# Decode attention with a gated MLP on one core: passing the opening barrier from a block late in the program

## The chip, the cores and the metric

One core of a Trainium2 chip. The metric is the device time of one execution in microseconds (us). A profiled execution also has a span, counted from the first recorded instruction; over 55 executions the time is 2.0 us above the span. In this document "last wo data" is the end of the last packet of the last weight load in the trace's packet records, and "first data" the start of the first packet of the first K load.

The engines, as the profile of before shows them: PE runs the matmuls (4482), DVE and ACT work on vectors (311 and 184 instructions), POOL fills constants (20), SP issues the loads. Each has a program of its own in the kernel; they meet at an opening barrier and then by semaphores. The packet records, sampled every microsecond from 5 to 1260 us, have exactly 16 packets under way at once, the fetches of code (queues 8 and 14) among them: one for each of 16 DMA engines.

## The reference, cut to what matters

```python
def reference(A_x, A_k_cache, A_v_cache, A_wq, A_wo, B_x, B_w1, B_b1, B_w2, B_b2, gate_w):
    ...
    x = A_x
    g = _sigmoid((x * gate_w).sum(-1, keepdims=True))
    a = _A_ref(x, A_k_cache, A_v_cache, A_wq, A_wo)   # 2 batches, 16 query heads on 8 KV heads, 32768 keys of 256
    b = _B_ref(x, B_w1, B_b1, B_w2, B_b2)             # 448 -> 1792 -> 448, gelu
    return g * a + (1 - g) * b
```

One new token per batch. The caches are 2 x 8 x 32768 x 256 bf16 values each, 537 MB together; the rest is small.

## The kernel before: the parts that matter

K and V tiles of 8.4 MB pass through a ring of three slots. SP's first K load is put into the entry block, ahead of the barrier; the five programs follow in blocks of their own.

```python
        entry = nc.main_func.blocks[-1]
        n0 = len(entry.instructions)
        engs["sp"].eng = nc.sync
        first_load(engs["sp"])
        ins = entry.instructions
        at = next(i for i, x in enumerate(ins) if x.engine == mybir.EngineType.SP and type(x).__name__ == "InstDrain")
        entry.instructions = ins[:at] + ins[n0:] + ins[at:n0]
        with nc.Block("main") as block:
            ...
            block.tensor(lambda eng: run("pe", eng))
```

PE's program is short in code: the 32 tiles are one loop, whose pass has a K half (scores) and a V half (weighted sum), each under a condition. Behind the loop come the last V tile in three pieces and the tail: 28 small matmuls for w2 (line L603) and 64 for wo (L781), which wait for wo's five pieces.

```python
            def tile(i):
                def k():
                    S(i)
                    next_slot()

                def v():
                    PV(i - LAG)
                    next_slot()

                E.iff(i < NTILES, lambda e: e.If_lt(R["i"], NTILES), k)
                E.iff(i >= LAG, lambda e: e.If_lt(R["n"], NTILES - 1), v)
                ...
            E.rep(NTILES + LAG - 1, tile)
            ...
            PV_pieces()
            ...
            TT()
            do_FB()
            E.wait("dve", "at")
            for i in range(len(WOP) - 1):
                FIN(i)
```

## Time and profile before

| | before |
|---|---|
| time, median of the first 3 executions | 1271.87 us (1271.77, 1271.87, 1272.60) |
| span of the profiled one | 1269.6 us |
| HBM read | 547.43 MB, 431 GB/s over the span |
| code fetches in the run | 16 KB at 52.9 us (q8), 8 KB at 140.3, 1226.1 and 1240.6 us (q14), 16 KB at 1265.8 us (q8) |
| last wo data | 1266.79 us |

How to read it: the DMA share was 1.00 from 50 to 1220 us, at 434 GB/s, and 0.98 from 1260 to 1265 us, and the last wo data ended 2.8 us before the end of the span. So look for what delays the DMA engines, or for what follows the last landing. The lines are shown in the prediction.

### The profile page before, as it was taken

How to read it: one execution, taken by the hardware profiler on the slowest of the kernel's cores; microseconds unless marked ns; L12 is line 12 of the kernel's file. 1: busy time of each engine (PE TensorE's matmuls, PEld its weight loads, DVE VectorE, ACT ScalarE, POOL GpSimd, SP SyncE). 2: the span in 40 equal slices, each digit the busy share in tenths (PEclk: the TensorE clock that was granted, in tenths of full speed). 3: DMA queues.
4: the chain of work that ended last, by engine and by line, in shares of the span. 5: the costliest groups of instructions: out<-in, count | busy, mean ns of one | idle time of the engine just before them, and what ended most of it. 6: DMA issues, size and time to landing. Idle time of an engine off the chain costs nothing.

```text
span 1269.6 us, 12680 instructions
## 1 busy us (share of the span) xinstructions
PE 870.9 (69%) x4482; PEld 179.4 (14%) x1938; DVE 688.8 (54%) x311; ACT 44.7 (4%) x184; POOL 4.6 (0%) x20
## 2 busy tenths in 40 slices
PE   0978677766688565785766877666876657857678
PEld 0211111111111111111111111111111111111113
DVE  4676536755356563556735467453575635656351
ACT  0100000000000000000000000000000000000000
POOL 1000000000000000000000000000000000000000
PEclk9889888877988788888778878888877789877789
DMA  9999999999999999999999999999999999999998
GB/s 407 451 429 429 432 429 438 438 440 432 429 432 432 429 434 440 436 438 429 432 432 429 432 440 438 436 432 429 434 429 429 440 438 438 432 429 432 432 428 367
DMA packets 11110, 547.50 MB, mean 431 GB/s; under 512 B 1369, under 2 KB 1633, under 8 KB 2145
## 3 DMA queue, kind: packets, MB, share of 16 engines
q1 hardware_dynamic: 10948, 547.43, 99.8%
q8 instruction: 2, 0.03, 0.0%
q10 hardware_dynamic: 156, 0.01, 0.0%
q14 instruction: 4, 0.02, 0.0%
HBM read 547.43 MB, written 0.00 MB: 431 GB/s over the span
## 4 chain that ended last, share of the span: by engine, by line
DMA 55%; PE 24%; DVE 14%; issue 6%; SPq 0%; ACT 0%; ACTq 0%
DMA ring<-in_A_k_cache_dram 51%; DVE ring L958 12%; PE ps_s L666 12%; PE ps_o L666 11%; DMA ring<-in_A_wo_dram 3%; DVE mx L962 1%; DMA PT<-in_gate_w_dram 1%; PE ps_m L721 0%; PE ps_m L716 0%; DVE gmax L964 0%; PE ps_o L577 0%; PE ps_o L445 0%; DVE gmx L968 0%; PE ps_o L548 0%; PE ps_o L582 0%
## 5 line engine op out<-in xcount | busy, mean ns | idle before, releaser
L958 DVE STREAM_TRANSPOSE ring<-ring 128x4096 uint32<-128x4096 uint32 x128 | 557.4, 4412 | 305.2 <-DMA ring<-in_A_k_cache_dram 304.9
L666 PE MATMUL ps_s<-ring,Abd 128*128 x2048 | 519.7, 416 | 221.1 <-DVE ring L958 220.9
L666 PE MATMUL ps_o<-ring,PT 128*24 x2048 | 271.5, 421 | 10.1 <-issue 9.9
L666 PEld LDWEIGHTS ps_s<-ring,Abd 128*128 x1024 | 106.2, 104 | 640.7 <-issue 637.7
L975 DVE STREAM_TRANSPOSE PT<-pexp 128x1024 bf16<-128x1024 bf16 x16 | 19.9, 1245 | 117.5 <-PE ps_o L666 117.5
L726 PE MATMUL ps_f<-o_sb,selg 128*32 128x257 f32 x30 | 15.5, 621 | 91.0 <-DVE o_sb L991 91.0
L666 PEld LDWEIGHTS ps_o<-ring,PT 128*24 x544 | 46.5, 90 | 214.9 <-issue 213.1
L962 DVE TENSOR_REDUCE mx<-ps_s 128x1 f32<-128x1024 f32 x16 | 19.6, 1225 | 63.5 <-PE ps_s L666 63.5
L874 ACT ACTIVATE negm<-ps_m 128x1 f32<-128x1 f32 x16 | 2.7, 171 | 1132.9 <-PE ps_m L721 1132.9
L991 DVE TENSOR_REDUCE o_sb<-ps_o 128x256 f32<-128x2048 f32 x15 | 34.4, 2291 | 0.5
L989 DVE TENSOR_TENSOR ps_o<-ps_o,mask 128x2048 f32<-128x2048 f32 x15 | 34.3, 2290 | 0.0
L716 PE MATMUL ps_m<-ident_f,mx 128*1 128x128 f32 x32 | 6.1, 270 | 22.3 <-DVE mx L962 22.3
L972 DVE COPY ls<-lsum 128x1 f32<-128x1 f32 x16 | 2.5, 154 | 33.4 <-ACT pexp L878 33.4
L548 PE MATMUL ps_o<-ring,xT 128*32 128x512 bf16 x16 | 5.6, 567 | 20.4 <-issue 20.4
L868 ACT COPY Abd<-qrep 32x16 bf16 (+1 forms) x128 | 19.5, 199 | 0.6
L619 PE MATMUL ps_s<-zeros 1*128 1x512 bf16 x32 | 15.7, 590 | 5.2 <-ACT Abd L868 2.7
L878 ACT ACTIVATE pexp<-ps_s,negm 128x1024 bf16<-128x1024 f32 x16 | 17.8, 1114 | 1.7
L619 PE MATMUL ps_o<-zeros 1*128 1x512 bf16 x64 | 17.3, 392 | 0.5 <-DVE o_sb L984 0.5
L726 PEld LDWEIGHTS ps_f<-o_sb,selg 128*32 128x32 f32 x30 | 2.7, 138 | 104.8 <-issue 104.8
L721 PE MATMUL ps_m<-ones_f,gmx 1*128 1x1 f32 x32 | 6.5, 270 | 11.1 <-DVE gmx L968 11.1
L964 DVE TENSOR_REDUCE gmax<-ps_m 1x2 f32<-1x128 f32 x16 | 4.5, 278 | 8.8 <-PE ps_m L716 8.8
L1005 DVE TENSOR_SCALAR o_sb<-ps_o,mask 128x256 f32<-128x256 f32 x1 | 0.5, 483 | 15.7 <-PE ps_o L666 15.7
(92 smaller groups left out, 81.4 us busy)
## 6 DMA issues: line engine op xcount, KB each, us to landing
ring<-in_A_v_cache_dram SPq DMA_DIRECT2D x1, 4096.0 KB, 27.2
ring<-in_A_v_cache_dram SPq DMA_DIRECT2D x2, 2048.0 KB, 33.9
ring<-in_A_wq_dram SPq DMA_DIRECT2D x1, 3072.0 KB, 28.8
ring<-in_B_w_dram SPq DMA_DIRECT2D x1, 1568.0 KB, 28.3
ring<-in_A_wo_dram SPq DMA_DIRECT2D x1, 1568.0 KB, 31.7
ring<-in_B_w_dram SPq DMA_DIRECT2D x1, 1344.0 KB, 32.3
ring<-in_A_wo_dram SPq DMA_DIRECT2D x1, 1008.0 KB, 33.7
ring<-in_A_wo_dram SPq DMA_DIRECT2D x1, 560.0 KB, 34.5
```

The costliest lines, as they stand in the source:

```text
L619: E.ins(lambda e: e.matmul(o, zeros[0:1, :], zero_x, start=True, stop=False, skip_group_check=True))
L666: return e.add_instruction(mybir.InstMatmult(name=f"I-{nc.next_id()}", engine=mybir.EngineType.PE, ldweights=None if load else False, ins= ...
L716: E.ins(lambda e: e.matmul(ps_m[0:1, C_MXT:C_MXT + P], mx[:, :], ident_f[:, :], start=True, stop=True), key=("M1", g))
L721: E.ins(lambda e: e.matmul(ps_m[:, C_BC:C_BC + 1], gmx[:, :], ones_f[0:1, 0:1], start=True, stop=True), key=("M2", g))
L726: E.ins(lambda e: e.matmul(ps_oa, selg[:, :], o_sb[:, :], start=False, stop=False, skip_group_check=True), key=("OT", g))
L868: E.ins(lambda e, o=o, Q=Q, c=c: e.copy(o[:, :, c:c + 2], qrep[32 * Q:32 * Q + 32, :, bass.ds(E.dyn(2 * g, 2), 2)]), key=(("A", g) if (Q = ...
L878: E.ins(lambda e: e.activation(pexp[:, :].rearrange("p (r i a) -> p i r a", r=CR, i=2), ps_s[:, :].rearrange("p (i r a) -> p i r a", i=2, ...
L958: E.ins(lambda e: e.transpose(k_words(idx, blk), k_words(idx, blk)), key=("T", idx, blk))
L962: E.ins(lambda e: e.tensor_reduce(mx[:, :], ps_s[:, :], AX.X, ALU.max), key=("MX", g))
L975: E.ins(lambda e: e.transpose(PT[:, :], pexp[:, :]), key=("PT", g))
L989: E.ins(lambda e: e.tensor_tensor(p, p, mb, ALU.mult), key=("OM", g))
L991: E.ins(lambda e: e.tensor_reduce(o_sb[:, 0:Dh], ps_o[:, :].rearrange("p (n d) -> p d n", d=Dh), AX.X, ALU.add), key=("OS", g))
```

## The change

The intent: four engines jump at once to a block that stands late in their program, pass the opening barrier there and jump back, so that late code is fetched at the start and not in the middle of the run or at its end.

```diff
+        def gate(eng, before):
+            ...
+            mine = [x for x in entry.instructions if of(x)]      # the engine's Drain, EventSemaphore, UnconditionalBranch
+            assert len(mine) == 3
+            name = f"gate_{eng.name}"
+            rest = [x for x in entry.instructions if not of(x)]
+            entry.instructions = rest + [mybir.InstUnconditionalBranch(
+                name=f"I-{nc.next_id()}", engine=eng, ins=[], outs=[], target=name)]
+            blocks = list(f.blocks)
+            at = next(i for i, b in enumerate(blocks) if b.name == before)
+            bb = mybir.BasicBlock(name=name, instructions=mine)
+            f.blocks = blocks[:at] + [bb] + blocks[at:]
+            ...
+        spots = [(ET.SP, names[-1]), (ET.Activation, names[last(ET.Activation)]), (ET.DVE, names[last(ET.DVE)]),
+                 (ET.PE, names[last(ET.PE) - 8])]
+        for eng, before in spots:
+            gate(eng, before)
```

SP, ACT and DVE get the block at their ends. PE gets it eight blocks before its end.

More of the change, by code (lines that the diff above doesn't have):

```diff
@@ L1073, in bass_gated_mix__gqa_block_cached__dense_activation_gelu__decode_kernel @@
             block.vector(lambda eng: run("dve", eng))
+        def gate(eng, before):
+            f = nc.main_func
+            of = lambda x: x.engine == eng and type(x).__name__ in ("InstDrain", "InstEventSemaphore", "InstUnconditionalBranch")
+            mine = [x for x in entry.instructions if of(x)]
[8 more added lines that the diff above has]
+            f.blocks = blocks[:at] + [bb] + blocks[at:]
+            nc.bb_map[name] = bass.BassBasicBlock(nc, bb, [eng], parent=nc.bb_map[entry.name])
+        blocks = list(nc.main_func.blocks)
+        names = [b.name for b in blocks]
+        ET = mybir.EngineType
+        last = lambda eng: max(i for i, b in enumerate(blocks[:-1]) if b.instructions[-1].engine == eng) + 1
+        spots = [(ET.SP, names[-1]), (ET.Activation, names[last(ET.Activation)]), (ET.DVE, names[last(ET.DVE)]),
+                 (ET.PE, names[last(ET.PE) - 8])]
+        for eng, before in spots:
+            gate(eng, before)
 _INS = ['A_x', 'A_k_cache', 'A_v_cache', 'A_wq', 'A_wo', 'B_x', 'B_w1', 'B_b1', 'B_w2', 'B_b2', 'gate_w']
```

## The prediction

> **What bounds the kernel now.** I read the page from the top down: first the DMA and GB/s rows of the 40 slices, then the queues, then the chain that ended last.
>
> ```profile
> DMA  9999999999999999999999999999999999999998
> GB/s 407 451 429 429 432 429 438 438 440 432 429 432 432 429 434 440 436 438 429 432 432 429 432 440 438 436 432 429 434 429 429 440 438 438 432 429 432 432 428 367
> ...
> q1 hardware_dynamic: 10948, 547.43, 99.8%
> q8 instruction: 2, 0.03, 0.0%
> ...
> q14 instruction: 4, 0.02, 0.0%
> HBM read 547.43 MB, written 0.00 MB: 431 GB/s over the span
> ...
> DMA 55%; PE 24%; DVE 14%; issue 6%; SPq 0%; ACT 0%; ACTq 0%
> ```
>
> The DMA row never falls below nine tenths until the last slice: the kernel streams the two caches once, and the stream is the bound. The two "instruction" rows are what this change is about: fetches of code during the run, on queues 8 and 14, next to the data of queue 1. They are 0.05 MB, so by bytes they are nothing.
>
> The table of busy time by stretch and the chain of waits show the same for the end:
>
> ```profile
> 50.00:1220.00 1170.00, 817.64 (x4081) 161.26 (x1665) 651.70 (x258) 37.38 (x165) 0.00 (x0) 0.83 1.00 434
> ...
> 1265.00:1266.00 1.00, 1.00 (x22) 0.71 (x16) 0.00 (x0) 0.00 (x0) 0.00 (x0) 1.00 0.69 249
> 1266.00:1267.00 1.00, 0.68 (x13) 0.36 (x11) 0.00 (x0) 0.00 (x0) 0.00 (x0) 1.00 0.09 33
> ...
> 1232.03 34.92 DMA ring<-in_A_wo_dram
> 1266.95 0.04 issue
> 1267.00 0.57 PE ps_f L781 x8
> 1267.57 0.02 issue
> 1267.59 0.38 DVE pexp L1044
> ```
>
> In a row of the first kind the last two numbers are DMA share and GB/s. The share is 1.00 for 1170 us and then falls to 0.69 and 0.09 in the last two microseconds: most of the 16 DMA engines are done and one or two are late. The last piece of wo waits for these, then come eight matmuls, a copy and the output. So the end is **the slowest DMA engine plus 2.8 us** (1266.8 to the span's 1269.6).
>
> To see which engine is late and why, I went to the packet records of the trace (start, duration, queue, size). They carry no engine number, but an engine's next packet starts 3 ns before the end of its previous one is noted, so the records sort into 16 chains. Result: from the first packets (1.04 to 1.87 us, one per engine) to 1265 us no chain has a hole over 60 ns, except at four instruction fetches:
>
> ```
> fetch starts us  took us  bytes  queue   what its engine's chain lost
>   52.89          1.06     16384  q8      1.55 us (hole 1.05, next 64 KB packet 2.92 instead of 2.42)
>  140.34          0.33      8192  q14     0.97 us (hole 0.31, next packet 3.08)
> 1226.06          0.31      8192  q14     0.69 us (hole 0.31, next packet 2.80)
> 1240.56          0.31      8192  q14     0.31 us
> 1265.79          1.09     16384  q8      on an engine that had finished its data, it seems
> ```
>
> As each engine always has backlog (K tiles land 43.8 us after their issue, though one needs 19.4 us), what a chain loses is never caught up. At the end the two chains that lost 1.55 and 0.97 us are the last: 1266.79 and 1266.66, the others 1265.1 to 1266.02. The weight of a fetch is therefore not its bytes over 431 GB/s but the full delay of one engine out of 16, for which all wait.
>
> [...]
>
> **The change part by part.**
> (1) It moves no data, no arithmetic and no wait. The order of instructions differs by one branch each on PE, DVE, ACT and SP: their three opening barrier instructions now stand late in their programs, so an engine jumps there, passes the barrier, and jumps back. The first K load stays in the entry block, ahead of SP's jump, at 0.00.
> (2) Cost at the start: four branches (a DVE or PE branch took 0.05 to 0.21 us) and the wait for up to four fetches under the first K load, an estimate of 2 to 5 us for the barrier, because a queued packet of 64 KB takes 2.42 us (3.0 to 3.5 the first time). What hangs on the barrier:
>
> ```profile
> 0.00 0.41 SPq L481 DMA_DIRECT2D ring<-in_A_k_cache_dram  x1
> ...
> 0.82 0.80 SPq L495 DMA_DIRECT2D ring<-in_A_wq_dram  x2
> ...
> 2.74 42.97 SPq L517 DMA_DIRECT2D ring<-in_A_k_cache_dram  x2
> ...
> 19.50 0.61 DVE L918 TENSOR_TENSOR gp_sb<-pexp,PT 2x448 f32<-2x448 bf16 x1 [9.38 <-DMA PT<-in_gate_w_dram]
> ...
> 22.30 17.42 DVE L958 STREAM_TRANSPOSE ring<-ring 128x4096 uint32<-128x4096 uint32 x4 [0.52 <-DMA ring<-in_A_k_cache_dram]
> ```
>
> wq is issued at 0.82 but its first packets run at 21.1, after the first K tile: 20 us of slack. The third K tile is issued at 45.7 and first needed at 52.9, and what releases its slot follows wq's landing, not the barrier. gate_w would land later by the barrier's delay, moving the first transposes from 22.3; they end at 39.7, and DVE's next thing on the path is the h copy at 45.3, so about 5.6 us are free, and PE's scores another 12 us before V0 is missed. The delay costs the stream nothing.
> (3) Gain: the fetches at 52.9 (PE), 140.3, 1226.1 and 1240.6 move to about 0.3 to 2 us. PE's gate stands eight blocks before its last, at about instruction 208 of 374 of the built program, so I take it that reaching there pulls in the block that was fetched at 52.9. Without any loss the chains would end thus: 1266.79 - 1.55 = 1265.24; 1266.66 - 0.97 = 1265.69; the 1226 one 1265.28; the last undisturbed one stays at 1266.02. Full gain in the stream: 1266.79 - 1266.02 = **0.77 us**.
> (4) What the fetches still cost at the start: 16 KB at the 27 GB/s of one engine (65536 B in 2.42 us) is 0.6 us, 8 KB 0.3 us, less what runs before that engine's first data at 1.1 to 1.9 us. The PE one fits below 1266.02 (1265.24 + 0.6), the 140 one just (1265.69 + 0.3 = 1265.99). So most of the gain should survive: my choice is 0.6.
> (5) Does PE pass it on? Its last stage does 92 small matmuls from 1262.32 at 0.048 us each, which would end at 1266.7 without waits; it ends at 1267.55 because it waits for wo pieces. That alone lets through 0.55. Tiles earlier in the stream also land sooner, so PE's chain before it moves too.
> Sum: 1271.87 - 0.6 = **1271.3 us**.
>
> **The rivals.**
> A. The fetch at the start lands in the middle of the first K packets and costs its engine as much as later (1.55 us happened under the same 64 KB packets). Then nothing is gained: 1271.9. For it: SP's K load is issued at 0.00, before or with the jumps. Against: data starts only at 1.04[...].
> B. [...] blocks are fetched twice, and the late ones again later: up to 1 us worse, 1272.5. Against: the loops show no refetching in 1100 us, so a few blocks do stay.
> C. The delayed barrier starves the stream at the start. The slacks of 20, 7 and 5.6 us speak against it; it would need a barrier beyond 6 us to show at all. 1273 and more.
> D. PE, not DMA, becomes the end: after 0.55 us nothing more comes through: 1271.3, which is no different from my number.
>
> **Range and chances.** Everything that I can find lies between -0.8 and +0.7 us; three runs of before spread over 0.8 us. So 1270.6 to 1272.3. 2% would be 25 us, and nothing here reaches it: same 0.99.
>
> **What would show it.** Right: the instruction fetches of 52.9, 140.3, 1226 and 1240.6 gone, records of the same size near 0 to 5 us; no chain with a hole after that; the last wo packet at 1266.0 to 1266.2; the 1266 to 1267 row with DMA share near zero. Step 2 right: barrier and wq issue some us later, the third K tile still at about 45.7 and no hole in the stream. Wrong: a chain that loses 1 us or more at the start (A), fetches after 50 us as before (B), a hole of all engines at 20 or 53 us (C). The number would also be wrong if the time outside the span (2.3 us now, 1271.87 against 1269.6) changed because the jumps come before the first recorded instruction.

The sum came to 1271.3 us: 1271.87, the median of before, less 0.6. 0.77, 0.6 and 0.55 us are worked out from the packet records and the matmul times that are quoted. That 434 GB/s is the most the stream can reach was not shown. That an engine waits at its jump for a fetch, on which the 2 to 5 us of step (2) rest, was an assumption.

## The result, and the profile after

| | before | changed |
|---|---|---|
| time, median of 6 | 1272.43 us (1271.77 to 1272.68) | 1273.20 us (1271.99 to 1273.45) |
| span of the profiled one | 1269.6 us | 1271.3 us |
| fetches between 10 and 1260 us | 4 | 0 |
| last wo data | 1266.79 us | 1267.24 us |
| last wo data to the end of the span | 2.8 us | 4.1 us |

The ratio is 1.0006 (95% interval 0.9993 to 1.0019): the same within 2%, and not told apart from no change. It is the ratio of the mean times of six runs each (1273.03 over 1272.30), so not quite that of the medians. The median of before had been 1271.87 when the prediction was made; three further executions moved it to 1272.43.

The queue rows of the page of the changed kernel, and the shares of the chain that ended last:

```profile
q8 instruction: 2, 0.03, 0.0%
...
q14 instruction: 3, 0.02, 0.0%
...
DMA 52%; PE 27%; DVE 15%; issue 6%; ACTq 0%; ACT 0%; DVEq 0%
```

The fetches are still there; DMA's share of the chain has fallen from 55% to 52% and PE's has risen from 24% to 27%. The packet records say where the fetches went:

```
fetch starts us  took us  bytes  queue   changed kernel
   4.10          0.32      8192  q14     next 64 KB packet of its DMA engine 2.83 instead of 2.42
   4.32          0.31      8192  q14     next packet 3.06
   4.42          1.20     16384  q8      its DMA engine is idle for data from 4.43 to 5.62, next packet 2.87
   6.72          0.31      8192  q14     next packet 2.71
1265.53          1.09     16384  q8
```

They moved, but none ran ahead of the data: three stand behind the first 64 KB packet of their DMA engine and one behind a second (first data at 1.01 us, first packets done at 4.05 to 4.86). The DMA engine of PE's fetch lost 1.19 us and then 0.45 us, 1.64 in all; the 8 KB fetches cost theirs 0.6 to 1.0 us each.

One engine did stand at the start. ACT's first DMA issue after the barrier, before and then in the changed kernel:

```profile
0.81 0.55 ACTq L836 DMA_DIRECT2D pexp<-in_A_x_dram  x1
```

```profile
1.41 4.44 ACTq L836 DMA_DIRECT2D pexp<-in_A_x_dram  x1
```

It took 4.4 to 4.7 us in each of the six profiles that have ACT's late block and the data ahead of the fetches, 2.2 to 2.3 in the two whose fetches ran ahead of the data, and 0.55 in gate_pe_only, where ACT has no late block. So the late block delays ACT; what ACT waits for there, no run shows. The stream did not feel it: gate_w's product on DVE ran at 21.51 us instead of 19.50, inside the slack that the prediction gives.

The end, from the chain of waits of the changed kernel:

```profile
1262.64 0.55 PE ps_m L791 x16
1263.19 2.54 PE ps_f L603 x28
1265.73 3.64 PE ps_f L781 x64
1269.39 0.38 DVE pexp L1044
```

Before, the last link ahead of the copies was wo's DMA (34.92 us to 1266.95); here it is PE alone, with all 92 small matmuls in a row. The table of busy time by stretch of the changed kernel tells why these took 6.2 us (the last three numbers of a row are granted TensorE clock, DMA share and GB/s):

```profile
1264.00:1265.00 1.00, 1.00 (x16) 0.70 (x12) 0.00 (x0) 0.00 (x0) 0.00 (x0) 0.50 0.98 392
1265.00:1266.00 1.00, 1.00 (x14) 0.73 (x12) 0.00 (x0) 0.00 (x0) 0.00 (x0) 0.50 0.65 231
1266.00:1267.00 1.00, 1.00 (x18) 0.76 (x16) 0.00 (x0) 0.00 (x0) 0.00 (x0) 0.63 0.09 34
1267.00:1268.00 1.00, 1.00 (x26) 0.92 (x22) 0.00 (x0) 0.00 (x0) 0.00 (x0) 1.00 0.02 5
```

The clock records put PE at 0.50 from 1263.33 to 1266.74 us in this execution, with 14 to 18 matmuls in a microsecond instead of 26. In the profile of before the clock was 1.00 from 1244.04 us to the end of the span. So three things have to be told apart: the fetches (theory A), something that makes PE late (theory B), and the clock (theory C).

For B there is a count: 12717 instructions against 12680. The block in PE's loop stands between two blocks that had followed each other without a jump; now each of the loop's passes needs one (PE's branches went from 489 to 521 in the trace; the median one took 0.207 us in both kernels).

### The profile page after: what moved, and what is told of

Its sections match the earlier page's. It is cut to its first block, busy times and chain, and to the rows that moved or that the text cites. A ratio compares the mean times of both kernels' runs of the same rounds, so it can differ in the third digit from the quotient of the medians. Undisturbed runs are those within 1.5% of the kernel's fastest.

```text
span 1271.3 us, 12717 instructions
## 1 busy us (share of the span) xinstructions
PE 866.7 (68%) x4482; PEld 179.6 (14%) x1938; DVE 688.5 (54%) x311; ACT 44.7 (4%) x184; POOL 4.6 (0%) x20
## 4 chain that ended last, share of the span: by engine, by line
DMA 52%; PE 27%; DVE 15%; issue 6%; ACTq 0%; ACT 0%; DVEq 0%
DMA ring<-in_A_k_cache_dram 51%; DVE ring L958 12%; PE ps_o L666 12%; PE ps_s L666 12%; DVE mx L962 1%; DMA PT<-in_gate_w_dram 1%; PE ps_m L716 0%; PE ps_m L721 0%; ACTq L836 0%; DVE gmax L964 0%; PE ps_o L577 0%; PE ps_o L445 0%; PE ps_f L781 0%; DVE gmx L968 0%; PE ps_o L548 0%
```

## The experiments

Eighteen kernels ran; all were correct. The theories, as the expectations name them: **A**, a code fetch under saturated DMA delays one of the 16 DMA engines, which stays late to the end; **B**, the added branch makes PE's tail late; **C**, the granted clock in the tail splits the executions of either kernel in two groups. The main rival of A is that fetches are harmless and the chains uneven for another reason.

### The changed kernel again, and its parts

**after_again**: no edit.

> The changed kernel once more, to tell what is of the kernel from what is of one execution. Theory A (a code fetch under saturated DMA delays one of the 16 DMA engines by 1.5 to 2 us, wherever in the stream it falls, and that delay stays to the end): again no fetch between 10 and 1260 us, the one of 16 KB near 4.4 us, one DMA engine's chain 1.5 to 2 us behind from there on, last wo data near 1267.2. Theory B (PE's tail sets the end because of one added branch of 0.17 to 0.23 us on each pass of PE's tile loop): PE's first small matmul of the w2 stage near 1263.1 again. Theory C (the extra time is the granted clock, 0.5 in 3.4 us of the tail by chance): the clock in the last 8 us may be 1.0 this time, and then the span is 1269.9 to 1270.3 instead of 1271.3; with 0.5 again, 1271.3.

Measured: five executions with spans of 1269.9, 1269.8, 1271.4, 1271.0 and 1271.3. The profiled one is of the short group: fetch of 16 KB at 4.24 us, last wo data 1267.11, w2 stage from 1263.01. The stretch of the tail and the end of its chain:

```profile
1262.00:1269.00 7.00, 5.21 (x108) 4.35 (x108) 0.99 (x3) 0.34 (x1) 0.00 (x0) 1.00 0.53 212
...
1232.29 34.99 DMA ring<-in_A_wo_dram
1267.28 0.04 issue
1267.33 0.57 PE ps_f L781 x8
```

Clock 1.00, and wo's landing is again the last link. So the same program ends by DMA or by PE, and the 1.4 us between its groups come with the clock. A, B and C as expected.

**gate_three**: PE keeps its barrier in the entry block.

```diff
-        spots = [(ET.SP, names[-1]), (ET.Activation, names[last(ET.Activation)]), (ET.DVE, names[last(ET.DVE)]),
-                 (ET.PE, names[last(ET.PE) - 8])]
+        spots = [(ET.SP, names[-1]), (ET.Activation, names[last(ET.Activation)]), (ET.DVE, names[last(ET.DVE)])]
```

> SP, ACT and DVE pass through their late blocks, PE does not. Theory A: the three fetches of 8 KB move to the start, PE's of 16 KB stays near 53 us and still costs its DMA engine about 1.55 us, so the last wo data lands near 1266.8 as before, and the time is that of the kernel before within 0.3 us. Theory B: no added branch, PE's w2 stage starts near 1262.3. If instead the 8 KB fetches were what costs, the last wo data would land near 1267.2.

Measured: 1272.06 us median of 5 (before in the same rounds 1271.82), 0.2 off and not told apart. The three 8 KB fetches are at 4.2, 4.3 and 6.7 us; PE's is at 55.5 us. Last wo data 1267.06, where 1266.8 was expected: by that number alone, one could blame the 8 KB fetches. The table further down decides it: the last data still comes a fixed time after the end of PE's fetch. PE reached the w2 stage at 1262.93, not at 1262.3; with no added branch, 0.26 us of that is the later landing of the last K tile; for the rest a different clock on the way (half clock for 3.4 us from 1221.1, before for 6.8 us from 1220.1) is likely, not shown.

**gate_pe_moved**: PE's block two places later, behind the tile loop.

```diff
-                 (ET.PE, names[last(ET.PE) - 8])]
+                 (ET.PE, names[last(ET.PE) - 6])]
```

> All four as in the changed kernel, but PE's late block stands two blocks later, behind its tile loop, so the loop has no added branch. Theory A: fetch of 16 KB near 4.4 us and the late chain as in the changed kernel, last wo data near 1267.2. Theory B: PE's gap between its last tile and the pieces is back from 1.21 to about 1.0 us or a little more (one branch at the exit), w2 stage near 1262.7; time 0.3 to 0.5 us below the changed kernel at equal clock. If the branch is irrelevant: w2 stage at 1263.1 as in the changed kernel.

Measured: 1272.35 us; last wo data 1267.37; w2 stage from 1263.24, later than expected, since its last K tile landed 0.2 us later than the changed kernel's. From the last transpose of PT to the last V tile's first matmul, which no landing disturbs, it took 18.14 us: between 18.39 in the changed kernel and 17.97 in the kernel before. The gap ahead of the last tile stayed at 1.21 us, where about 1.0 was expected. The five spans are 1269.9, 1270.1, 1270.2, 1270.7 and 1270.9; the longer two are some 0.5 us below the changed kernel's long executions (1271.0 to 1271.4), as B expected; their clock was not profiled.

**branch_only**: the kernel before, with a block at the changed kernel's place in PE's loop, reached once at PE's end; it holds PE's last two instructions, one of them a wait that was added to PE's program for this (first line of the cut).

```diff
+            E.wait("pool", "ts1")
...
+        at = last(ET.PE) - 8
+        tail = blocks[last(ET.PE) - 1]
+        end = list(tail.instructions)
+        bb = mybir.BasicBlock(name="pad_PE", instructions=end[-2:])
+        tail.instructions = end[:-2] + [mybir.InstUnconditionalBranch(
+            name=f"I-{nc.next_id()}", engine=ET.PE, ins=[], outs=[], target="pad_PE")]
+        nc.main_func.blocks = blocks[:at] + [bb] + blocks[at:]
```

> The kernel before plus one block in PE's tile loop at the place of the late block, passed once at the very end; barrier untouched. Theory B: 33 more branches, PE's gap before the pieces 1.2 instead of 0.99 us, w2 stage near 1262.7 (0.4 later than before), the fetches where they were before (53, 140, 1226, 1240 us), last wo data near 1266.8. The time is above that of before by 0 to 0.5 us. If the branch is irrelevant: w2 stage at 1262.3.

Measured: that stretch took 18.43 us, 0.46 more than before, with 32 more branches. From the timelines, before first, PE's gap ahead of the last V tile:

```profile
1248.21 0.87 PE L666 MATMUL ps_o<-ring,PT 128*24 x5 [0.99 <-issue]
```

```profile
1248.84 0.38 PE L666 MATMUL ps_o<-ring,PT 128*24 x1 [1.21 <-issue]
```

The bracket is the idle time ahead of the row: 0.99 against 1.21 us. The stretch has two passes of the loop's end, hence 2 x 0.2. The time did not move: 1271.84 us median of 5 (1271.60 to 1271.98), all in the short group, where PE waits for wo anyway. So B is real, 0.42 to 0.46 us of PE time in the tail. That it shows in the end only where PE ends last is argued: no profile has a long execution with this edit.

**gate_pe_only**: PE alone passes through its block.

```diff
-        spots = [(ET.SP, names[-1]), (ET.Activation, ...), (ET.DVE, ...), (ET.PE, names[last(ET.PE) - 8])]
+        spots = [(ET.PE, names[last(ET.PE) - 8])]
```

> Only PE passes through its late block. In the changed kernel PE's fetch of 16 KB and one of 8 KB seem to stand back to back on one DMA engine (4.10 to 5.63 us, hole 1.52). Theory A: with PE alone the hole is 1.05 to 1.25 us, plus 0.4 us on the next packet, at about 4.2 us; the 8 KB fetches are back at 140, 1226 and 1240 us; last wo data 1266.7 to 1267.0; PE's gap before the pieces 1.2 us (branch in the loop). Time like before at clock 1.0 in the tail.

Measured: fetch at 4.64 us; the hole of its DMA engine is 0.90 us and the next packet 2.93 us instead of 2.42, together 1.41 us (1.64 in the changed kernel). The expectation misread that kernel: a data packet follows the 8 KB fetch of 4.10 on its DMA engine at 4.41 us, so PE's fetch stood on another one, alone. Last wo data 1267.19, above the expected range: this time PE's fetch fell on a DMA engine whose first packet ended later (4.65 us; 4.43 in the changed kernel). 1272.89 us median of 5, spans 1270.0, 1270.0, 1270.8, 1270.9, 1271.0. The long three have the branch in the loop and are hardly longer than gate_pe_moved's, which do not: so few executions do not split the long group's 0.6 us into branch and landing.

### Fetches ahead of the data

**k0_late_before**: the first K load behind SP's barrier, no late blocks.

```diff
-        at = next(i for i, x in enumerate(ins) if x.engine == mybir.EngineType.SP and type(x).__name__ == "InstDrain")
+        at = next(i for i, x in enumerate(ins) if x.engine == mybir.EngineType.SP and type(x).__name__ == "InstEventSemaphore") + 1
```

> The kernel before with the first K load issued by SP behind the opening barrier instead of ahead of it. Control for the next run: the stream starts 0.6 to 0.8 us later, the fetches stay at 53, 140, 1226 and 1240 us, so last wo data minus first data stays at 1265.7 to 1265.9 us and the time (from the first instruction) depends on where the span then begins.

Measured: first data 1.78 us, last wo data 1267.80, difference 1266.03 (a little above the expected range); fetches where they were; 1272.56 us median of 5 (before in the same rounds 1272.72).

**k0_late_after**: the same edit in the changed kernel.

> The changed kernel with the first K load behind SP's barrier in the late block, so that the code fetches are asked for before any data is queued. Theory A (what a fetch costs is the delay of one saturated DMA engine): the fetches run ahead of the first 64 KB packets, no chain loses more than 0.6 us, and last wo data minus first data falls from 1266.1 to 1266.2 us to 1265.0 to 1265.4 us; the later start of the stream (0.7 to 1.1 us) gives about the same back. Rival (the code fetches do not matter, the chains are uneven for another reason): the difference stays at 1265.8 to 1266.2 us, and the kernel is 0.7 to 1.1 us slower than the changed one.

This one missed its aim. The late blocks are cut out of the entry block afterwards, and the load stayed in it: SP's instructions came out as in the changed kernel, first data at 1.03. It counts as five more executions of the changed kernel: spans 1270.3, 1269.9, 1271.1, 1269.9, 1269.9. The profile has PE's fetch at 4.84 us, alone on its DMA engine (1.02 us hole, next packet 0.51 us slower), and last wo data at 1267.57.

**k0_in_gate**: the load really inside SP's late block.

```diff
+        g = next(b for b in nc.main_func.blocks if b.name == "gate_SP")
+        g.instructions = list(g.instructions)[:2] + late + list(g.instructions)[2:]     # late: the first K load
```

> The changed kernel with the first K load really behind SP's barrier, inside the late block (the run called k0_late_after left it at 0.0 us, first data at 1.03, so it was the changed kernel once more). Theory A: the code fetches are asked for at about 0.6 us, the first data packets come at about 2.1 us instead of 1.0; if the fetches run ahead of them, no chain loses more than 0.6 us and last wo data minus first data is 1265.0 to 1265.5 us, where the changed kernel has 1266.1 to 1266.5 and the kernel before 1265.7 to 1266.2. Rival: the difference stays at 1266.0 to 1266.5.

Measured: the fetches run from 0.88 to 2.81 us and the first data comes at 3.28, so all are done. SP's issue of the load:

```profile
0.85 1.81 SPq L481 DMA_DIRECT2D ring<-in_A_k_cache_dram  x1
```

It took 1.81 us instead of the 0.41 of before, while the fetches were under way; whether these made it longer, no run shows. From first to last data 1264.58 us: 1.2 us less than before and 1.6 less than in the changed kernel (1265.75 and 1266.23), and below the range that A gave. No DMA engine's chain has a hole over 61 ns in between. A stands, its rival falls. The kernel itself is slower, 1274.67 us median of 4: the stream starts 2.2 us later, and at 1264.07 us a half-clock step fell into the tail (0.50 from 1265 to 1267 us).

**k0_in_gate_wait** and its control **k0_wait_before**: SP also waits for POOL's memset of Abd (`engs["sp"].wait("pool", "A0")` ahead of the load), with the late blocks and without.

> The same, and SP also waits for a memset of the pool engine that ends near 3.9 us, so that no data can stand in front of the code fetches: first data near 5 us. Theory A: all four fetches are done by 3 us, no chain has a hole between first data and 1260 us, last wo data minus first data is 1264.9 to 1265.4 us, 0.7 to 1.4 us less than in the changed kernel; the whole is about 3 us slower than it because the stream starts 4 us late. Rival (uneven chains have another cause): the difference stays at 1266.0 to 1266.5 us.

> Control for k0_in_gate_wait: the kernel before with the same late first load and no late blocks. Theory A: fetches at 53 to 57, 140, 1226 and 1240 us as before (shifted by the late start), one chain loses 1.5 us, last wo data minus first data 1265.7 to 1266.3 us, so 0.5 to 1.2 us more than k0_in_gate_wait. Rival: no difference between the two.

Measured: first to last data 4.53 to 1269.29, 1264.76 us, with the blocks; 4.42 to 1270.16, 1265.73 us, without. The pair differs by 0.98 us in the stream, with the fetch of 16 KB at 1.63 us in the one and at 58.67 us in the other. The times are 1275.54 and 1275.08 us: the one with the shorter stream is the slower, as its profile again has a half-clock step in the tail (1265.21 to 1268.62) and its control has none; one execution of four, with a span of 1272.0, is shorter than all of the control's (1272.9 to 1273.2).

### The last data follows PE's fetch

With all profiles at hand, one subtraction tests A without sorting packets into chains: last wo data minus the end of PE's 16 KB fetch.

| run | fetch ends, us | last wo data, us | difference, us |
|---|---|---|---|
| before | 53.95 | 1266.79 | 1212.84 |
| before_again | 54.34 | 1267.21 | 1212.87 |
| before_look1 | 54.29 | 1267.12 | 1212.83 |
| before_look2 | 54.16 | 1266.99 | 1212.83 |
| before_look3 | 53.94 | 1266.77 | 1212.83 |
| before_look6 | 53.93 | 1266.75 | 1212.82 |
| branch_only | 54.05 | 1266.87 | 1212.82 |
| before_look4 | 56.68 | 1267.12 | 1210.44 |
| before_look5 | 56.45 | 1266.88 | 1210.43 |
| gate_three | 56.62 | 1267.06 | 1210.44 |
| k0_late_before | 57.37 | 1267.80 | 1210.43 |
| k0_wait_before | 59.74 | 1270.16 | 1210.42 |
| changed kernel | 5.63 | 1267.24 | 1261.61 |
| after_again | 5.49 | 1267.11 | 1261.62 |
| after_look | 5.74 | 1267.39 | 1261.65 |
| k0_late_after | 5.88 | 1267.57 | 1261.70 |
| gate_pe_moved | 5.72 | 1267.37 | 1261.65 |
| gate_pe_only | 5.56 | 1267.19 | 1261.63 |

Within a group the difference holds to 0.1 us while the last data itself varies by up to 3.3 us; the second group's fetch stands one 64 KB packet later (2.40 us between groups, a packet takes 2.42). So in all 18 profiles with PE's fetch in the stream, the DMA engine that served it reads as the one that ends last. The rest of the variation is mostly which DMA engine this is: their first packets end anywhere from 3.9 to 5.0 us.

### Two groups of executions

**before_again**, **before_look1** to **before_look6** and **after_look**: the two kernels without an edit.

> The kernel before once more. Theory C (two modes of the tail by the granted clock): executions fall in two groups of span, 1269.6 to 1269.9 and 1270.5 to 1270.9; the profiled one has clock 1.0 throughout the last 8 us if it is of the first group and 3.4 us at 0.5 if it is of the second. If spans spread evenly, theory C falls.

> The kernel before, one profile. Theory C (the group of spans 0.9 us longer is the clock in the tail, in this kernel as in the changed one): a span of 1269.6 to 1270.1 with clock 1.0 from 1260 to 1268 us, or one of 1270.4 to 1271.0 with clock 0.5 for 3.4 us in there, and then PE, not wo's landing, releases the last copies. Rival: a span of the longer group with full clock in the tail.

> The kernel before, one profile more, in search of one of the longer group. Theory C: a span of 1270.4 to 1271.0 has the granted clock at 0.5 for 3.4 us between 1260 and 1268 us; a span of 1269.5 to 1270.1 has 1.0 there. Rival: a longer span with full clock in the tail.

> The same kernel and the same expectation as the two looks before it: the group of the span and the clock between 1260 and 1268 us go together (theory C), or they do not (rival).

> The changed kernel, one more profile. Theory C: 1269.8 to 1270.3 at full clock in the tail, 1271.0 to 1271.4 with 3.4 us at 0.5. Theory A: last wo data at 1261.15 us + the end of the first packet on the DMA engine that serves PE's fetch + what that engine loses there (hole plus slower next packet), within 0.2 us, as in the nine profiles so far.

before_again and the first five looks at the kernel before were of the short group (spans 1269.5 to 1270.0), all at clock 1.0 in the tail. So was after_look (1270.2), with last wo data at 1267.39 where A's sum gave 1267.27. before_look6 was of the long group, 1270.5. Its tail, in one stretch and in the chain:

```profile
1262.00:1269.00 7.00, 6.52 (x107) 5.08 (x103) 0.60 (x2) 0.34 (x1) 0.00 (x0) 0.76 0.51 205
...
1262.36 2.41 PE ps_f L603 x28
1264.77 3.78 PE ps_f L781 x64
...
1268.57 0.38 DVE pexp L1044
```

Half clock (0.50) from 1262.64 to 1266.06 us, and PE ends last although the last data had landed early, at 1266.75. C holds for both kernels. Over all executions with a listed span:

| | before | changed |
|---|---|---|
| short group | 25 of 38, mean 1269.75 us | 8 of 17, mean 1269.98 us |
| long group | 13 of 38, mean 1270.70 us | 9 of 17, mean 1271.27 us |
| difference, short / long | | +0.22 / +0.57 us |

(k0_late_after counted as the changed kernel; the line between the groups is 1270.35. After the first comparison the runs lie on five chips, and the kernel before has both groups on four of them.) Whether the change makes long executions more frequent is open: 34% and 53% of so few executions do not tell.

No version beat both kernels. Fetching ahead of the data shortens the stream by 1.0 to 1.6 us and costs more than 2 us of later start.

## Why the prediction was wrong

Predicted was 1271.3 us with a range to 1272.3; measured 1273.20.

- **The bound before, and what a fetch weighs: right.** The stream is the bound at full clock, and the slowest of 16 DMA engines sets its end; k0_in_gate, its waiting pair and the table of differences show it. (Its 2.3 us outside the span mixed two executions: the profiled one took 1271.53 us, so 1.9 to 2.0.)
- **Step (2), the barrier: wrong size, no effect on the stream, as said.** The estimate was 2 to 5 us. PE's barrier semaphore came at 1.12 instead of 0.75 us, 0.37 later: the jumps did not wait for the fetches, which ran at 4.1 us and later. ACT stood instead, 4.44 us in its first issue. wq was issued at 1.43 instead of 0.82, the third K tile at 47.25 instead of 45.38 us (the prediction's 45.7 is the end of that issue), and no hole of all engines followed, so rival C fell.
- **Step (3), which fetches move: right in kind, wrong in time.** All four left the middle of the run and none came back, so rival B fell. They were put at "about 0.3 to 2 us", ahead of or beside the first data; they ran at 4.1 to 6.7, behind first packets of 3 us. The 16 KB fetch at 1265.5 stayed in both kernels.
- **Step (4), what they still cost at the start: this is the step that failed.** It said 0.6 us for 16 KB and 0.3 for 8 KB, from 27 GB/s. Measured in the four profiles of the changed program: 1.64, 1.76, 1.69 and 1.53 us on the DMA engine of PE's fetch, against 1.55 before. 16 KB of code took 1.0 to 1.3 us, not 0.6, and the packet after it was 0.4 to 0.5 us slower; for 8 KB it was 0.6 to 1.0 us in all. Nothing of it ran before the first data. That is rival A, named and not chosen. Last wo data is 1267.33 on the mean of those four profiles and 1266.95 on that of eight of before: 0.37 us later instead of 0.77 earlier. Of the 0.37, about 0.1 is the larger loss and 0.1 the later end of that DMA engine's first packet (4.46 against 4.38 us on the mean); the rest stays open.
- **Step (1), "one branch each": wrong for PE.** The comparison of the programs showed the new block's branch in the midst of PE's loop, and I read it as passed once. It separates two blocks that had been neighbours, so each pass takes a jump; 0.42 us in the tail.
- **Step (5) and rival D: the clock was left out.** 92 matmuls at 0.048 us hold at clock 1.0. In the long group they need 5.97 us from the first to the last one's start, in both kernels, and then the end is PE's: 1263.12 against 1262.29 for its start (before_look6), 0.83 us later, which is 0.45 of later landing of the last K tile, 0.42 of branches and -0.04 of other differences. The three times of before (1271.77, 1271.87, 1272.60) already were of two groups, and I took the gap for scatter. The range was drawn too low as well: +0.7 us on 1271.87 is 1272.6, and rival B was put at 1272.5, both above its end of 1272.3.

So, as far as 38 and 17 executions tell, the change costs 0.2 us in one group and 0.6 in the other. The median difference of 0.8 in the first comparison is these plus more long executions (5 of 6 for the changed kernel), which more executions did not confirm as a property of it. Of the miss of 1.9 us, 0.56 is the median of before itself, 0.6 the gain that did not come, and 0.77 the measured loss.

Why the half-clock step falls into the tail of some executions, no run controlled, but the traces narrow it down. In the first profiles of both kernels (88 and 91 clock records) all steps within the span lie 3.413 us or a multiple of it apart, the shortest stretch at 0.5 is 3.41 us, and where the steps lie against the kernel differs: a stretch at 0.5 began at 1233.80 us before and at 1232.61 us in the changed kernel. Continued at that distance, these points cut the tail into windows of 3.41 us; of the changed kernel (first line) and the kernel before, around the pause in which PE waits for DVE's end of the last tile:

```profile
1259.91:1263.33 3.42, 1.42 (x25) 0.81 (x26) 1.76 (x5) 0.00 (x0) 0.00 (x0) 1.00 0.98 409
...
1257.69:1261.10 3.41, 2.11 (x11) 0.84 (x10) 1.09 (x3) 0.00 (x0) 0.00 (x0) 1.00 0.99 419
1261.10:1264.52 3.42, 2.68 (x62) 2.49 (x64) 0.78 (x3) 0.00 (x0) 0.00 (x0) 1.00 0.99 410
```

In the first the pause lies in one window, with PE busy for 1.42 us, and the half clock begins at that window's end; in the second it is divided. The four profiles with a step in the tail have 1.41 to 1.45 us in the window before it; in the other 16 no window that begins between 1256 and 1265 us has less than 1.78. In mid-stream (six profiles looked through), windows of 1.4 to 1.8 us went either way. So the two went together in 20 tails; a rule or a threshold is not shown.

## What to carry to other kernels

Here all 16 DMA engines were busy from the first microseconds (first packets at 1.01 to 1.87 us), and a small transfer behind the first packet had no cheap place: the 16 KB of code cost their DMA engine 1.53 to 1.76 us at the start of the changed program, 1.55 in the middle of the run before. In such a kernel look at the slowest DMA engine, not at bytes over bandwidth, and do not count on a fetch being cheaper at the start. A block put between two blocks of a loop turned a fall-through into a jump (32 more branches on PE, 0.42 to 0.46 us in the tail), so compare instruction counts of the traces. Where two ends lie within half a microsecond of each other, take several profiles of the kernel before and see whether its times have groups (here two, 0.95 us apart on the mean).
